# Zero matmuls in three places at the start of a fused attention and MLP kernel

## The chip, the cores and the metric

The kernel runs on one core of a Trainium2 chip. The metric is the device time of one execution in microseconds (us), as the median of several runs. The engines of a core are named as in the profile: PE (TensorE, matmuls; PEld are its weight loads), DVE (VectorE), ACT (ScalarE), POOL (GpSimd) and SP (SyncE, which here only issues DMAs).

## The reference

Two layers follow each other. The first is linear attention with decay, per batch (4) and head (8), over 768 positions with 64 channels. It works in blocks of 64 positions and carries a state from block to block:

```python
for b in range(nb):
    intra = np.einsum('bhic,bhjc->bhij', qb, kb) * Dmask[None]
    intra = np.einsum('bhij,bhjd->bhid', intra, vb)
    inter = np.einsum('bhid,bhde->bhie', qb * lam_pow[None], kv_state)
    out[:, :, sl] = intra + inter
    kb_dec = kb * rev_pow[None]
    kv_state = lam_block[None, :, None, None] * kv_state + np.einsum('bhsd,bhse->bhde', kb_dec, vb)
```

The second is an MLP on the 3072 tokens, with all heads of a token side by side (512 channels), a hidden width of 2048 and an ELU between:

```python
h = x @ w_in
g = np.where(h > 0.0, h, alpha * (np.exp(np.minimum(h, 0.0)) - 1.0))
return (g @ w_out).astype(np.float32)
```

Inputs and the output are fp32.

## The kernel before

The kernel cuts the sequence in six chunks of 128 positions instead of twelve of 64, so there are 24 pieces of work g = 4 c + b (chunk c of batch b), each with all eight heads and 128 tokens. Pieces 0 to 3 go through the MLP alone, later ones in pairs. Arithmetic on PE is fp16 with fp32 sums.

The steps of one piece have one letter each:

- T (att_T_pe, line 262): eight PE transposes turn q and k so that channels are on partitions; DVE multiplies q by the decay on the way out of PSUM (qT, line 278), ACT copies k (kT, line 279).
- S (att_S, line 282): eight matmuls of kT with qT give the scores; DVE multiplies them by the decay mask (pp, line 306).
- P (att_P, line 315): the product with v (line 326) and, for later chunks, with the state (line 332). ACT or DVE copies the sum to xt (line 347 or 349).
- U (att_U, line 376): the state's update from kd (k times decay, made by POOL in att_kd, line 157) and v, written to st by DVE (line 404 or 406); M (att_M, line 356) lets POOL decay the old state (stt, line 366).
- 1:g:j (mm1, line 455): 16 or 8 matmuls of one fourth (or one eighth) of w_in with xt into a bank psH, of which there are two; ACT makes exp and relu of it (lines 472 and 473), DVE joins both to g (line 445).
- 2:g:j (mm2, line 478): four matmuls of g with four slices of w_out, summed in psM; after the last, ACT copies the result (osb) and SP stores it.

The order is written out by hand. Each engine works through its instructions in the order in which the program gives them, and the program runs the tokens of the string OPEN (line 51) in order: first memsets of the states (z, Z), then T0, T1, S0, S1, P0, P1, T2, 1:0:0, S2, 1:1:0, P2, U0, M, 1:2:0, 1:0:1, 2:0:0 and so on. Behind OPEN a small planner places the rest by fixed lags. FIRST (line 50) comes before OPEN and has the cast of q of piece 0 (q0:0) and the decay constants (c0 to c2).

Loads are in POOL_ORDER (line 45), on POOL's DMA queue, which also casts fp32 to fp16: k0, k1, the two iota, q1, k2, v1, i0, v0 and so on, where i0 to i7 are pairs of 128-column slices of w_in and o0 to o7 pairs of 128-row slices of w_out. d0 to d3 in this list are the kd products of POOL, m4 the decay of the first state; POOL works these in order with its DMA issues, so a load behind d0 is issued after d0. q of piece 0 alone comes as fp32 on SP's queue (raw_q, line 105) and is cast by DVE (line 115).

PSUM banks go by name: BANKS (line 62) gives the bank of each early step, and mm1 takes the two banks psH in turn.

What stands ahead of the first PE work on DVE: the casts of iota (lines 204 to 206), the identity matrix (208), the causal mask (211), small copies (216, 217), the cast of q0 (115).

Of the kernel before, what the change touches and what calls it, by code (L numbers as in the profile page):

```python
# [7 lines left out]
FP32 = mybir.dt.float32  # L8
FP16 = mybir.dt.float16
# [6 lines left out]
def kernel(  # L16
# [11 lines left out]
    nc = tc.nc  # L28
# [20 lines left out]
    RAW = "q0"  # L49
    FIRST = "q0:0 c0 c1 c2"  # L50
    OPEN = (
        "z1 z0 z3 Z1 Z2 Z0 z2 T0 T1 S0 S1 P0 P1 T2 1:0:0 S2 1:1:0 P2 U0 M 1:2:0 1:0:1 2:0:0 "
        "1:1:1 2:1:0 1:2:1 T3 2:2:0 1:0:2 S3 1:2:2 2:2:1 2:1:1 P3 1:1:2 1:3:0 2:0:1 2:0:2 "
        "2:1:2 1:1:3 U1 1:2:3 M Z3 2:2:2 1:3:2 U2 1:3:1 2:1:3 1:0:3 T5 T4 2:2:3 1:3:3 S4:5 "
        "2:0:3 2:3:2 2:3:0 M U3 M B:P4:P5:U4:U5 W8 2:3:3 1:4:1 T6 W9 1:4:0 T7 2:3:1 1:4:3 S6:7 "
# [14 lines left out]
    cpool = ctx.enter_context(tc.tile_pool(name="cst", bufs=1))  # L70
    wpool = ctx.enter_context(tc.tile_pool(name="w", bufs=1))
    asb = ctx.enter_context(tc.tile_pool(name="asb", bufs=1))
    msb = ctx.enter_context(tc.tile_pool(name="msb", bufs=1))
    ps = ctx.enter_context(tc.tile_pool(name="ps", bufs=1, space=bass.MemoryType.PSUM))

    lam_b = cpool.tile([128, H], FP32, name="lam_b")
    nc.sync.dma_start(out=lam_b[:], in_=lam.unsqueeze(0).broadcast_to([128, H]))
# [32 lines left out]
    def cast_raw(g, w, eng):  # L110
        n = f"{w}{g}"
        t = asb.tile([128, 1, H, 64], FP16, tag=f"{w}n1", name=f"{w}n{g}", bufs=4)
        (qg if w == "q" else kg)[g] = t
        if eng == 0:
            nc.vector.tensor_copy(t[:, 0], raw[n][:])  # L115
        else:
            nc.scalar.copy(t[:, 0], raw[n][:])
# [164 lines left out]
    def att_S(g):  # L282
        qt, kt = qkT[g]
        psS[g] = [
            bank(f"S{g}", hh, [128, NHP, 128], FP32, f"psS{g}_{hh}") for hh in range(2)
        ]
        for hp in range(NHP):
            for hh in range(2):
                r = slice(hh * 64, (hh + 1) * 64)
                nc.tensor.matmul(  # L290
                    psS[g][hh][:, hp, :], lhsT=kt[r, hp, :], rhs=qt[r, hp, :],
                    start=True, stop=True,
                )
# [7 lines left out]
    def att_E(g):  # L301
        pts = psS.pop(g)

        def half(hh):
            P = asb.tile([128, NHP, 128], FP16, tag="pp", name=f"pp{g}_{hh}", bufs=6)
            nc.vector.tensor_tensor(  # L306
                out=P[:], in0=pts[hh][:], in1=mask[:, hh::2, :], op=ALU.mult
            )
            Pt[(g, hh)] = P
            if hh == 1:  # L310
                E_done.add(g)

        return [lambda: half(0), lambda: half(1)]
# [62 lines left out]
    def att_U(g, pu=None):  # L376

        cb, b = divmod(g, B)
        if cb == NCB - 1:
            return []  # L380
        vt = of(vg, g)
        if pu is None:
            full = bank(f"U{g}", 0, [128, NHP, 128], FP32, f"psU{g}")
            for hp in range(NHP):
                nc.tensor.matmul(
                    full[:, hp, :].rearrange("p (h e) -> p h e", h=2),
                    lhsT=kds[g][:, 2 * hp : 2 * hp + 2, :],
                    rhs=vt[:, 2 * hp : 2 * hp + 2, :], start=True, stop=True,
                )
        else:  # L390
            for hp in range(NHP):
                for hh in range(2):
                    r = slice(hh * 64, (hh + 1) * 64)
                    nc.tensor.matmul(  # L394
                        pu[r, hp, :], lhsT=kds[g][:, 2 * hp + hh, :], rhs=vt[:, 2 * hp + hh, :],
                        start=True, stop=True, skip_group_check=True,
                    )
        new = st[b][(cb + 1) % 2]

        def update(hh):  # L400
            r = slice(hh * 64, (hh + 1) * 64)
            src = full[r, :, r] if pu is None else pu[r, :, :]
            if cb == 0:
                nc.vector.tensor_copy(new[r, :, r], src)
            else:
                nc.vector.tensor_tensor(  # L406
                    out=new[r, :, r], in0=stt.pop((g, hh))[r], in1=src, op=ALU.add
                )
            if hh == 1:
                Y_done.add(g)  # L410

        return [lambda: update(0), lambda: update(1)]

    def burst(*ops):

        us = [int(o[1:]) for o in ops if o[0] == "U" and int(o[1:]) // B < NCB - 1]
        evs, i = [], 0
        for o in ops:
            if o[0] == "P":
                evs += att_P(int(o[1:]))  # L420
            elif int(o[1:]) in us:
                if i == 0:
                    pu = bank(o, 0, [128, 2, NHP, 64], FP32, f"psU{o[1:]}")
                evs += att_U(int(o[1:]), pu[:, i])
                i += 1
        if evs:
            late.insert(0, evs[0])
            late.pop(0)()
            late.extend(evs[1:])
# [91 lines left out]
    def ready(t):  # L521

        g = int(t[1:])
        if t[0] == "P":
            assert g < B or f"U{g - B}" in seen
        if t[0] == "U" and g < 2 * B:
            assert f"{'z' if g < B else 'Z'}{g % B}" in seen
        if t[0] == "U" and g >= B:
            assert f"U{g - B}" in seen and (g < 2 * B or f"P{g - B}" in seen)
        seen.add(t)  # L530

    def run(t):
        w, *a = t[0], *t[1:].replace(":", " ").split()
        if w == "B":
            for o in a:
                ready(o)
            burst(*a)
            return
        a = [int(x) for x in a]
        if w in "PUzZ":  # L540
            ready(t)
        if w == "S":
            for g in a:
                att_S(g)
            for g in a:
                late.extend(att_E(g))
            late.pop(0)()
            late.pop(0)()
        elif w == "P":
            burst(t)  # L550
        elif w == "U":
            late.extend(att_U(*a))
            while late:
                late.pop(0)()
        else:
            {"T": att_T_pe, "1": mm1, "2": mm2, "Z": zero_st, "z": zero_st1,
             "q": lambda g, e: cast_raw(g, "q", e), "k": lambda g, e: cast_raw(g, "k", e),
             "c": lambda i: (emit_qs, emit_mask, emit_ks)[i](), "W": pool_work, "L": load_pair,
             "M": next_M}[w](*a)

    for t in FIRST.split():
        run(t)
# [30 lines left out]
    for x, (g, j) in enumerate(m1):  # L593
# [3 lines left out]
        n = 2  # L597
# [6 lines left out]
    for t in prog:  # L604
        run(t)
# [33 lines left out]
```

## Time and profile before

| what | value |
|---|---|
| median of three runs | 218.0 us (217.15 to 218.4) |
| span of the profiled execution, first to last instruction | 215.9 us |
| the profiled execution's own time beside its span | not given; the median is 2.1 us above the span |
| PE busy | 199.9 us (93%) |
| PEld busy | 138.2 us (64%) |
| DVE and ACT busy | 129.9 and 129.1 us (60% each) |
| POOL busy | 96.2 us (45%) |
| chain that ended last | PE 83%, DMA 7%, POOL 6% |
| PE's idle time before its first instruction | 5.58 us |

The page of a profile gives one execution. Busy time is that in which an engine had an instruction at work; matmuls overlap, so a busy PE isn't yet PE at its peak. The timeline merges neighbouring instructions of one line, operation and shape to a row: start, length, engine, line, what is written from what, the count, and in brackets how long the engine had been idle and what ended it. The chain is followed back from the last instruction: at each step to what released it, or to the instruction before it on its engine. Views of waits give sums of idle time by what ended it. A DMA's time is that from issue to landing.

### The profile page before, as it was taken

To read this page: it belongs to the slowest core of one execution; us is meant where nothing else is said; L and a number is where in the kernel's file an instruction comes from. 1 tells how busy PE (TensorE), PEld (TensorE's weight loads), DVE (VectorE), ACT (ScalarE), POOL (GpSimd) and SP (SyncE) were. 2 spreads that over 40 slices of the span, in tenths; PEclk is the share of its full clock that TensorE was granted. 3 is DMA by queue.
4 is the path that set the end of the run, shared out by engine and by line. 5 is a ranking of instruction groups with operands and counts; after the bars stand their busy time and mean duration, and the time that the engine had idled before them with its cause. 6 is when DMAs were issued, how large, how long until landed. Compare 5 with 4: busy or idle time off the path is not lost.

```text
span 215.9 us, 5095 instructions
## 1 busy us (share of the span) xinstructions
PE 199.9 (93%) x2036; PEld 138.2 (64%) x2036; DVE 129.9 (60%) x223; ACT 129.1 (60%) x245; POOL 96.2 (45%) x115
## 2 busy tenths in 40 slices
PE   0568999999999998999999999999999999999992
PEld 0466676768685675666766766766766666766641
DVE  3926463777837778658657657667667547444410
ACT  4536664884866656665565566476476576566730
POOL 7998890999996419167067159300000000000000
PEclk9999999999999999999999999999999999999999
DMA  8999999999999956989969919999114110111021
GB/s 89 140 173 193 190 144 180 139 169 144 151 156 145 143 126 131 123 109 97 153 114 125 175 58 103 152 181 152 50 59 90 52 49 0 55 49 49 3 92 54
DMA packets 101976, 24.59 MB, mean 114 GB/s; under 512 B 92608, under 2 KB 99008, under 8 KB 101952
## 3 DMA queue, kind: packets, MB, share of 16 engines
q0 software_dynamic: 79760, 13.50, 82.6%
q1 hardware_dynamic: 22192, 10.76, 25.6%
q8 instruction: 16, 0.26, 0.5%
q14 instruction: 8, 0.07, 0.1%
HBM read 27.27 MB, written 6.29 MB: 155 GB/s over the span
## 4 chain that ended last, share of the span: by engine, by line
PE 83%; DMA 7%; POOL 6%; issue 1%; DVE 1%; ACT 0%; SPq 0%; POOLq 0%
PE psM L488 38%; PE psH L466 36%; DMA wo<-in_moe_w_out_dram 4%; DMA kT<-kn 3%; PE psO L326 3%; PE psS L290 3%; PE psO L332 2%; POOL wi L136 1%; POOL kn L97 1%; POOL vn L97 1%; POOL qn L97 1%; PE psT L271 1%; PE psU L394 1%; POOL kd L162 0%; POOL wo L143 0%
## 5 line engine op out<-in xcount | busy, mean ns | idle before, releaser
L466 PE MATMUL psH<-xt,wi 128*128 128x256 f16 (+1 forms) x896 | 99.9, 259 | 1.5 <-DVE g L445 0.8
L445 DVE SCALAR_TENSOR_TENSOR g<-e,psH 128x512 f16<-128x512 f32 x96 | 65.8, 686 | 56.5 <-ACT psH L473 55.9
L488 PE MATMUL psM<-wo,g 128*128 128x512 f16 (+1 forms) x388 | 96.4, 377 | 0.9 <-DVE osb L501 0.5
L472 ACT ACTIVATE e<-psH 128x512 f32<-128x512 f32 x96 | 57.3, 597 | 66.1 <-PE psH L466 62.8
L466 PEld LDWEIGHTS <-wi 128*128 128x128 f16 x896 | 77.8, 99 | 26.8 <-DVE g L445 2.0
L473 ACT ACTIVATE psH<-psH 128x512 f32<-128x512 f32 x96 | 57.0, 594 | 0.0
L488 PEld LDWEIGHTS <-g 128*128 128x128 f16 x388 | 36.3, 98 | 29.9 <-issue 1.3
L306 DVE TENSOR_TENSOR pp<-psS,mask 128x512 f16<-128x512 f32 x48 | 30.9, 684 | 5.3 <-PE psS L290 5.3
L162 POOL TENSOR_TENSOR kd<-kn,ks 128x512 f16<-128x512 f16 x20 | 20.7, 1039 | 18.7 <-DMA kn<-in_k_dram 17.7
L366 POOL TENSOR_TENSOR stt<-st,upp 64x256 f32<-64x256 f16 x32 | 19.5, 608 | 19.8 <-DVE st L406 13.5
L503 ACT COPY osb<-psM 128x512 f32<-128x512 f32 (+1 forms) x24 | 13.9, 581 | 6.3 <-PE psM L488 6.3
L97 POOL DMA_DIRECT2D kn<-in_k_dram x14 | 15.5, 1106 | 0.8 <-POOLq L623 0.8
L97 POOL DMA_DIRECT2D vn<-in_v_dram x14 | 15.5, 1109 | 0.6 <-DMA wi<-in_moe_w_in_dram 0.6
L326 PE MATMUL psO<-pp,vn 128*64 128x128 f16 x192 | 12.4, 230 | 3.0 <-DMA vn<-in_v_dram 2.9
L97 POOL DMA_DIRECT2D qn<-in_q_dram x13 | 14.8, 1139 | 0.0
L406 DVE TENSOR_TENSOR st<-stt,psU 64x256 f16<-64x256 f32 x32 | 13.3, 417 | 1.2 <-PE psU L394 0.5
L326 PEld LDWEIGHTS <-vn 128*64 128x64 f16 x192 | 10.1, 114 | 6.1 <-DMA vn<-in_v_dram 3.1
L349 DVE TENSOR_TENSOR xt<-psO,qs 128x512 f16<-128x512 f32 x16 | 11.0, 688 | 4.1 <-PE psO L332 4.1
L332 PE MATMUL psO<-qT,st 128*64 128x128 f16 x160 | 10.0, 219 | 0.0
L271 PE MATMUL psT<-ident,qn 128*128 128x128 f16 x32 | 3.8, 252 | 6.5 <-DVE qn L115 5.6
L290 PE MATMUL psS<-qT,kT 64*128 64x128 f16 x192 | 8.7, 228 | 0.8 <-DMA kT<-kn 0.7
L332 PEld LDWEIGHTS <-st 128*64 128x64 f16 x160 | 8.9, 110 | 0.0
(38 smaller groups left out, 64.8 us busy)
## 6 DMA issues: line engine op xcount, KB each, us to landing
out_dram<-osb SPq DMA_DIRECT2D x23, 256.0 KB, 2.5
kn<-in_k_dram POOLq DMA_DIRECT2D x10, 256.0 KB, 8.1
qn<-in_q_dram POOLq DMA_DIRECT2D x10, 256.0 KB, 7.1
vn<-in_v_dram POOLq DMA_DIRECT2D x10, 256.0 KB, 8.6
wi<-in_moe_w_in_dram POOLq DMA_DIRECT2D x8, 256.0 KB, 7.4
wo<-in_moe_w_out_dram POOLq DMA_DIRECT2D x8, 256.0 KB, 8.4
kn<-in_k_dram POOLq DMA_DIRECT2D x4, 128.0 KB, 4.3
vn<-in_v_dram POOLq DMA_DIRECT2D x4, 128.0 KB, 6.1
```

Source lines behind the costliest of these rows:

```text
L97: nc.gpsimd.dma_start(out=t[:].rearrange("p b h d -> p (b h) d"), in_=src)
L162: nc.gpsimd.tensor_tensor(out=kd[:], in0=of(kg, g), in1=ks[:].unsqueeze(2).broadcast_to([128, H, 64]), op=ALU.mult,)
L290: nc.tensor.matmul(psS[g][hh][:, hp, :], lhsT=kt[r, hp, :], rhs=qt[r, hp, :], start=True, stop=True,)
L306: nc.vector.tensor_tensor(out=P[:], in0=pts[hh][:], in1=mask[:, hh::2, :], op=ALU.mult)
L326: nc.tensor.matmul(po[r, hp, :], lhsT=vt[:, 2 * hp + hh, :], rhs=Pt[(g, hh)][:, hp, :], start=True, stop=(cb == 0), skip_group_check=True,)
L332: nc.tensor.matmul(po[r, hp, :], lhsT=st[b][cb % 2][:, hp, r], rhs=qt[:, hp, :], start=False, stop=True, skip_group_check=True,)
L366: nc.gpsimd.tensor_tensor(out=tmp[r], in0=old[r, :, r], in1=upp[r].unsqueeze(2).broadcast_to([64, NHP, 64]), op=ALU.mult,)
L445: nc.vector.scalar_tensor_tensor(out=g[:].rearrange("p f c t -> p (f c t)"), in0=e[:], scalar=-1.0, in1=r[:], op0=ALU.add, op1=ALU.min,)
L466: nc.tensor.matmul(pH[:, f * n * 128 : (f + 1) * n * 128], lhsT=wi16[i][:, kk, w * 128 : (w + 1) * 128], rhs=xg[g0][:, kk, :], start=(kk = ...
L472: nc.scalar.activation(e[:], pH[:], AF.Exp)
L473: nc.scalar.activation(pH[:], pH[:], AF.Relu)
L488: nc.tensor.matmul(psM[g][:, cols], lhsT=gts[(g, j * FB + f)], rhs=wo16[i][:, w, cols], start=first and f == 0, stop=end and f == FB - 1, ...
```

## The change

A tile zero16 of 128 x 512 fp16 zeros is made by DVE ahead of everything else that the kernel gives DVE. A function zero_matmuls(n) takes a psH bank and issues n matmuls of 512 columns with zeros as both operands; nothing reads their sums. Ten are issued at the very start, two between T0 and T1 (token w2), and six between S1 and P0 (token w6). All other instructions keep their order.

```diff
     OPEN = (
-        "z1 z0 z3 Z1 Z2 Z0 z2 T0 T1 S0 S1 P0 P1 T2 1:0:0 S2 1:1:0 P2 U0 M 1:2:0 1:0:1 2:0:0 "
+        "z1 z0 z3 Z1 Z2 Z0 z2 T0 w2 T1 S0 S1 w6 P0 P1 T2 1:0:0 S2 1:1:0 P2 U0 M 1:2:0 1:0:1 2:0:0 "
...
     ps = ctx.enter_context(tc.tile_pool(name="ps", bufs=1, space=bass.MemoryType.PSUM))
+
+    zero16 = cpool.tile([128, 512], FP16, name="zero16")
+    nc.vector.memset(zero16[:], 0.0)
+
+    def zero_matmuls(n):
+        z = ps.tile([128, 512], FP32, tag="psH", bufs=2, name="psZ")
+        for _ in range(n):
+            nc.tensor.matmul(z[:], lhsT=zero16[:, 0:128], rhs=zero16[:], start=True, stop=True)
+
+    zero_matmuls(10)
 
     lam_b = cpool.tile([128, H], FP32, name="lam_b")
...
-             "M": next_M}[w](*a)
+             "M": next_M, "w": zero_matmuls}[w](*a)
```

## The prediction

> **What bounds the kernel now.** I read the page first: TensorE (PE) is busy 199.9 of 215.9 us, so the question for a change at the start is whether PE or something else sets the time there. So next came the timeline of the first 31 us (columns: start us, length us, engine, line, operation, tiles, shape, count, and in brackets the idle time before and what ended it):
>
> ```profile
> 5.58 0.61 PE L271 MATMUL psT<-ident,qn 128*128 128x128 f16 x4 [5.58 <-DVE qn L115]
> 7.51 0.61 PE L271 MATMUL psT<-ident,qn 128*128 128x128 f16 x4 [0.90 <-DMA qn<-in_q_dram]
> ...
> 12.70 1.06 PE L326 MATMUL psO<-pp,vn 128*64 128x128 f16 x16 [2.87 <-DMA vn<-in_v_dram]
> ...
> 14.53 1.91 PE L466 MATMUL psH<-xt,wi 128*128 128x128 f16 x16
> ...
> 19.77 2.13 PE L466 MATMUL psH<-xt,wi 128*128 128x128 f16 x32 [0.71 <-ACT xt L347]
> ...
> 22.67 0.59 PE L488 MATMUL psM<-wo,g 128*128 128x512 f16 x2 [0.34 <-DMA wo<-in_moe_w_out_dram]
> ...
> 23.10 1.05 PE L466 MATMUL psH<-xt,wi 128*128 128x128 f16 x16
> ```
>
> Two things are to be seen. PE has three holes, and the change puts zeros in exactly these: 5.58 us ahead of chunk 0, 0.90 ahead of chunk 1 and 2.87 ahead of P0. And PE starts slow: the same 16 matmuls of 128 columns take 1.91 us at 14.53 and 1.05 at 23.10. One slow matmul lasts 0.314 us and a fast one 0.219 (largest and smallest of the tile view of psT), so the step from one start to the next is (1.91 - 0.31)/15 = 0.107 us slow and (1.05 - 0.22)/15 = 0.055 fast. At 19.77 it is already fast. The granted clock reads 1.00 in all stages, so that column does not show the slow phase; the durations do.
>
> Then the chain that ended last, around the end of this stage (start us, length us, what):
>
> ```profile
> 12.57 1.04 POOL kd L162
> 13.61 0.90 POOL qn L97
> 14.51 8.12 DMA wo<-in_moe_w_out_dram
> 22.63 0.04 issue
> 22.67 0.59 PE psM L488 x2
> 23.26 0.89 PE psH L466 x16
> 24.15 0.86 PE psM L488 x4
> 25.02 0.89 PE psH L466 x16
> ```
>
> Up to 22.63 the chain is not PE at all. It is POOL, issuing loads one behind the other, and then the second pair of w_out (o1), issued at 14.51 and landed 8.12 us later; behind 22.67 it is PE, piece against piece. The third matmul of the step 2:0:0 had waited for o1. So a PE that is earlier before 22.67 waits longer there.
>
> Last, whether a later load binds as well: the weight loads between 34 and 37 us, and POOL's own idle time in its first 60 us (us in total, times, longest):
>
> ```profile
> 36.02 0.90 PEld L466 LDWEIGHTS <-wi 128*128 128x128 f16 x16 [0.51 <-DMA wi<-in_moe_w_in_dram]
> ```
>
> ```profile
> POOL stt L366 <- DVE st L404: 5.4, 1, 5.4
> POOL kn L97 <- POOLq L623: 0.8, 1, 0.8
> POOL vn L97 <- DMA wi<-in_moe_w_in_dram: 0.6, 1, 0.6
> POOL kd L162 <- DMA kn<-in_k_dram: 0.5, 1, 0.5
> ```
>
> i6, issued at 27.94 and landed 8.0 us later (35.97), releases the step 1:1:3 at 36.02; PE's matmuls before it run to 36.00. That is a second date that transfers set, with 0.02 us of slack. POOL waits in this time for DMA (queue room, the landing of kn3 ahead of d3) and once for PE's work, 5.4 us up to 37.85, behind the second date. The first 36 us are paced by loads.
>
> **The change part by part.** The memset of zero16 is 1 KB per partition, as those of st: 0.27 us (group of L188, 272 ns). VectorE does nothing before 3.60, where it waits for iota; the memset hides there. Uncovered it would cost 0.27.
>
> The ten matmuls of 512 columns: at the slow step 4 x 0.107 = 0.43 us each, 4.3 in all. Other engines begin at 0.73 (ScalarE, SyncE); a memset from there ends at 1.0 and the block at 5.3, 0.3 before T0's data at 5.58. If it ran over by some tenths, T0's readers are still later: ScalarE's kT copy at 7.18 and VectorE's qT at 7.67 come behind their own queues, while T0 ends at 6.6. Cost 0.
>
> w2: T0's last matmul starts at 6.30, so PE is free at 6.41; two slow ones end at 7.26, T1's data come at 7.47. Cost 0. w6: S1's last pair starts at 9.52, so it runs from 9.63 for 6 x 0.43 = 2.6 us slow (to 12.2) or 6 x 0.22 = 1.3 fast (to 10.9); v lands at 12.66. Cost 0, even at the slow step. The products are ready by then (VectorE's four pp end at 11.6). The tile psZ takes three turns of the two psH banks; PE alone writes it and nobody reads it, so the next psH step waits for no other engine. No DMA is added, moved or held; POOL's and SyncE's queues are the same. 18 matmuls and 18 weight loads more on PE: code loading is not seen to stop PE in this trace, taken at 0.
>
> What a warm clock gives. In this trace the fast step comes near 17.2 us (within the row at 16.91), 4.5 us after PE began to work without long holes at 12.70. By that measure ten zeros (4.3 us) and T0 make it fast by about 6 to 7 us. Now the walk of the changed kernel, with fast pieces from the chain (0.34 per P of 8, 0.45 per T, 0.89 per 16 of mm1, 0.33 per S). P0 and P1 from 12.70 to 13.4. T2 13.5 to 14.0, since q2 lands at 13.49 (issued 7.71, 5.8 us). 1:0:0 half at 14.0, half when i1 lands (8.58 + 6.3 = 14.9), to 15.3; before, 16.2. S2 to 15.7, 1:1:0 to 16.6, P2 behind VectorE's two pp (15.8 + 1.3 = 17.1) to 17.3, U0 to 17.5. xt2 on ScalarE behind four exp and relu of 0.6 (15.5 + 2.4 = 17.9) to 18.5; before, 19.7. 1:2:0 to 19.45, 1:0:1 behind i3 (11.62 + 8.0 = 19.6) to 20.4, the first two of 2:0:0 to 20.9; before, 22.3. So PE gains 1.4 us at this place, of 1.9 that the halved pieces promise (0.5 in P0 and P1, 0.4 in T2, 0.9 in 1:0:0, 0.1 in S2 and the start of 1:1:0). And there it stands until 22.67: the wait for o1 grows from 0.34 to 1.7 us, and this is what is late next. From 22.67 on every piece of PE already runs at 0.86 to 0.89, with nothing slow to win.
>
> Can o1 land earlier? Its issue follows d0 (12.57) and q3 (13.61) on POOL, and POOL asks PE for nothing before stt at 21.84; so no. Can the start of loads move? The first issue at 1.25 waits 0.8 for POOL's own queue. The memset might meet it at SBUF; bounds: below, 0 (it ends 0.2 before), above, its whole 0.27. Taken: 0.
>
> One cost the trace doesn't show is what a wait of 1.7 us does to the fast clock: the longest PE waits while fast are 0.7 and 0.8 us, and behind them the pieces are still 0.87. From above, the slow phase again: 4.5 us at half rate, +2.2 us, as at 12.70 to 17.2. From below, 0. I take 0, since 1.7 is nearer to 0.8 than to the 5.6 us of idle before the slow start.
>
> The Trainium skill, "TensorE: Matmul & The Clock Gate" (Part 1), says that the clock opens after about 3.4 us of sustained work and closes after an idle window of 3.4 us, and that the ramp is worth under 1% of a kernel. It agrees with the steps of 0.107 and 0.055; by it the zeros open the clock and a wait of 1.7 us leaves it open. Its 1%, an estimate from that page, would be 2.2 us off; my sum by the rows is 0, since the loads take it.
>
> Sum: span 215.9 + 0 (zeros and memset) - 1.4 (fast pieces) + 1.4 (longer wait for o1) = 215.9. The three runs have a median of 218.0; the 2.1 between lie outside the span or in the spread of the runs (the profiled execution's own time is not given). Forecast 218.0, no change; its own range is the spread of the runs, 217.2 to 218.6.
>
> **The rivals.**
> (a) The loads come earlier in timed runs than under the profiler. Then the wait for o1 is not there and the 1.4 us show, if i6 lands as much earlier; with half of it, 0.7. For it: the wait is only 0.34, and the profile records every packet. Against: two dates bind one behind the other, and 218.0 leaves no room for a timed run that is much shorter than the profiled one. 216.6.
> (b) The other side: the clock closes in the longer wait for o1 (20.9 to 22.67). PE is the chain from there on, so a second slow phase counts in full: +2.2, 220.2. It decides if 1.7 us of idle suffices to close it. If instead it closes in the 1.8 us before P0, PE is as before and nothing changes.
> (c) The change doesn't do what it says: the zeros do not open the clock (or not for long), the fast step comes near 17 us again. All zeros still fit in their holes: 218.0.
>
> **How the numbers follow.** Forecast 0.62, (c) 0.14, (a) 0.14, (b) 0.10. A median of three or so can be told from no change at about 0.5% (1.1 us). Same: 0.62 + 0.14, less 0.05 for noise on both sides, and 0.03 from the halves of (a) that stay within it: 0.74. Faster: 0.11 of (a) and 0.04 = 0.15. Slower: 0.10 of (b) and 0.01 = 0.11. The range leaves out (b) and the outer half of (a): 216.7 to 218.9, where 218.9 has the 0.27 of the memset above 218.6.
>
> **What would show it.** Right: row times fall in 1:0:0 from 1.91 to about 1.3 with a hole for wi in it; P0 still begins near 12.7; the idle time before the third psM matmul is 1.2 to 2 us, released by DMA wo, at 22.6 again; 1:1:3 at 36.0; span within 0.5 of 215.9. Wrong: psM's third matmul clearly before 22.2 (a), steps of 0.107 behind 22.7 (b), or at 14.5 (c), or P0 later than 12.9, zeros in the way. I'd be wrong altogether if the landings of o1 and i6 moved with PE's work.

## The result

The changed kernel takes 216.96 us (median of 22 executions, 215.59 to 217.93), the kernel before, in executions taken between them, 218.76 (217.0 to 223.66). The ratio of the two is 0.9945, with a 95% interval of 0.9926 to 0.9964; so the change makes the kernel faster by 0.4 to 0.7%, some 1.2 us. The time lies inside the forecast range, but the forecast was "no change". The ratios leave out executions that are more than 1.5% above the fastest of the same kernel, which is why 0.9945 is nearer to 1 than the medians are: of all executions told of here, 21 of 178 of the kernel before and none of 46 of the changed kernel took over 220 us, and in the 17 whose granted clock is on record it had closed for a while (mean 0.992 or less; the last section shows such a closing in profiles of other kernels).

In the executions whose span is on record the time is 1.7 to 2.0 us above it. The two profiled spans are 215.9 before and 215.5 after: one profile of each can't carry a difference of 1.2 us, and this is the difficulty of the whole case.

The timeline of PE in the first 25 us of the changed kernel (start us, length us, engine, line, operation, tiles, count, and in brackets the idle time before and what ended it):

```profile
1.19 4.45 PE L82 MATMUL psZ<-zero 128*128 128x512 f16 x10 [1.19 <-DVE zero L77]
5.58 0.61 PE L281 MATMUL psT<-ident,qn 128*128 128x128 f16 x4
...
6.26 0.59 PE L82 MATMUL psZ<-zero 128*128 128x512 f16 x2
7.83 0.40 PE L281 MATMUL psT<-ident,qn 128*128 128x128 f16 x4 [0.98 <-DMA qn<-in_q_dram]
...
9.46 1.47 PE L82 MATMUL psZ<-zero 128*128 128x512 f16 x6
12.46 0.64 PE L336 MATMUL psO<-pp,vn 128*64 128x128 f16 x16 [1.54 <-DMA vn<-in_v_dram]
...
13.76 0.61 PE L476 MATMUL psH<-xt,wi 128*128 128x128 f16 x8
14.63 0.62 PE L476 MATMUL psH<-xt,wi 128*128 128x128 f16 x8 [0.26 <-DMA wi<-in_moe_w_in_dram]
...
15.51 1.07 PE L476 MATMUL psH<-xt,wi 128*128 128x128 f16 x16
...
20.68 0.62 PE L476 MATMUL psH<-xt,wi 128*128 128x128 f16 x8 [0.63 <-DMA wi<-in_moe_w_in_dram]
...
22.61 0.59 PE L498 MATMUL psM<-wo,g 128*128 128x512 f16 x2 [0.88 <-DMA wo<-in_moe_w_out_dram]
23.04 1.05 PE L476 MATMUL psH<-xt,wi 128*128 128x128 f16 x16
```

The zeros fit in their holes: T0 begins at 5.58 as before, P0 at 12.46 (before 12.70). The clock opens during them: T1's four transposes take 0.40 us (0.61 before) and 1:1:0 takes 1.07. The trace's clock record puts the opening at 6.08 us; in the profile of before it is at 17.18. And the idle time ahead of the third psM matmul has grown from 0.34 to 0.88 us. That matmul starts at 22.61, against 22.67.

The chain there, and the weight loads of 1:1:3:

```profile
13.61 0.90 POOL qn L107
14.50 8.06 DMA wo<-in_moe_w_out_dram
22.56 0.04 issue
22.61 0.59 PE psM L498 x2
23.20 0.89 PE psH L476 x16
24.09 0.86 PE psM L498 x4
```

```profile
35.70 0.95 PEld L476 LDWEIGHTS <-wi 128*128 128x128 f16 x16 [0.26 <-DMA wi<-in_moe_w_in_dram]
```

The same two dates: o1 lands at 22.56 (22.63 before), and the step of i6 begins at 35.7 (36.0). POOL's waits in its first 60 us tell the same, the long one for PE's work is shorter, 4.7 instead of 5.4 us, and the one for queue room longer:

```profile
POOL stt L376 <- DVE st L414: 4.7, 1, 4.7
POOL vn L107 <- DMA wi<-in_moe_w_in_dram: 1.9, 1, 1.9
POOL kn L107 <- POOLq L633: 0.8, 1, 0.8
```

In this pair of profiles, then, the change brings 0.25 us by 36 us (the first matmul of 1:1:3 starts at 35.77 instead of 36.02). Where do 1.2 us come from? PE's next long wait is near 70 us, where the second half of the scores of pieces 10 and 11 waits for kT. kT is made there by a DMA transpose on SP's queue. The waits of PE between 55 and 76 us (us in total, times, longest), before and after:

```profile
PE psS L290 <- DMA kT<-kn: 0.7, 1, 0.7
```

```profile
PE psS L300 <- DMA kT<-kn: 0.5, 1, 0.5
```

### The profile page after: what moved, and what is told of

The parts are those of the page before. It is cut to its first block, busy times and chain, and to the rows that moved or that the text cites. A ratio compares the mean times of both kernels' runs of the same rounds, so it can differ in the third digit from the quotient of the medians.

```text
span 215.5 us, 5132 instructions
## 1 busy us (share of the span) xinstructions
PE 203.4 (94%) x2054; PEld 137.8 (64%) x2054; DVE 130.1 (60%) x224; ACT 129.1 (60%) x245; POOL 96.1 (45%) x115
## 4 chain that ended last, share of the span: by engine, by line
PE 83%; DMA 7%; POOL 6%; issue 1%; DVE 1%; ACT 0%; SPq 0%; POOLq 0%
PE psM L498 38%; PE psH L476 36%; DMA wo<-in_moe_w_out_dram 4%; DMA kT<-kn 3%; PE psO L336 3%; PE psS L300 3%; PE psO L342 2%; POOL wi L146 1%; POOL kn L107 1%; POOL vn L107 1%; POOL qn L107 1%; PE psT L281 1%; PE psU L404 1%; POOL kd L172 0%; POOL wo L153 0%
## 5 line engine op out<-in xcount | busy, mean ns | idle before, releaser
L482 ACT ACTIVATE e<-psH 128x512 f32<-128x512 f32 x96 | 57.3, 597 | 66.4 <-PE psH L476 63.2
L476 PEld LDWEIGHTS <-wi 128*128 128x128 f16 x896 | 77.0, 98 | 27.7 <-DVE g L455 2.0
L107 POOL DMA_DIRECT2D vn<-in_v_dram x14 | 15.5, 1109 | 1.9 <-DMA wi<-in_moe_w_in_dram 1.9
L107 POOL DMA_DIRECT2D kn<-in_k_dram x14 | 15.5, 1106 | 0.8 <-POOLq L633 0.8
L300 PE MATMUL psS<-qT,kT 64*128 64x128 f16 x192 | 8.1, 218 | 0.9 <-DMA kT<-kn 0.5
L357 ACT CAST xt<-psO 128x512 f16<-128x512 f32 x8 | 4.4, 588 | 6.9 <-PE psO L336 4.8
```

The source lines that it names most:

```text
L107: nc.gpsimd.dma_start(out=t[:].rearrange("p b h d -> p (b h) d"), in_=src)
L300: nc.tensor.matmul(psS[g][hh][:, hp, :], lhsT=kt[r, hp, :], rhs=qt[r, hp, :], start=True, stop=True,)
L476: nc.tensor.matmul(pH[:, f * n * 128 : (f + 1) * n * 128], lhsT=wi16[i][:, kk, w * 128 : (w + 1) * 128], rhs=xg[g0][:, kk, :], start=(kk = ...
L482: nc.scalar.activation(e[:], pH[:], AF.Exp)
```

## The experiments

The expectations speak of four theories.

- **A**: the clock opens at another time in each execution. In some of them it opens late, PE and not o1 sets the start of 22.6, and the zeros pay. Otherwise the dates of the loads bind, as forecast.
- **B**: the loads land earlier in timed executions than in profiled ones, so that the early clock shows (rival (a) of the prediction).
- **C**: something else that varies between executions, or noise.
- **D** (formed after the third group): it is not the clock. The added instructions on PE shift the code packets, 16 KB that PE's queue of instructions fetches now and then; the fifth of them, near 61 us, no longer meets the DMA transposes that PE waits for near 70.

Ratios are to the kernel before on the same chip, with 95% intervals, over 10 to 12 executions each (6 for light_after; before_3 and before_4 are one execution each and have no ratio). "Average" below means that of the executions under 220 us, worked out from the single times.

### One part at a time, beside an unchanged kernel

before_again is the kernel before, a measure of the comparison itself. The others are made from the changed kernel:

```diff
 memset_only:  -    zero_matmuls(10)
               -  T0 w2 T1 S0 S1 w6 P0      +  T0 T1 S0 S1 P0
 ten_only:     -  T0 w2 T1 S0 S1 w6 P0      +  T0 T1 S0 S1 P0
 w6_only:      -    zero_matmuls(10)
               -  T0 w2 T1 S0 S1 w6 P0      +  T0 T1 S0 S1 w6 P0
```

> The kernel before, unchanged, as a second sample of its start. Theory A (late opening): the moment at which PE's step falls from 0.107 to 0.055 us differs from execution to execution, and in many it comes later than the 17.2 us of the first profile, by up to some 3 us; PE then passes the landing of o1 and everything behind is late by up to 1 us. Expected: ratio 1.000, the spans of the runs spread over 2 us or more, and a second profile whose fast step does not begin at 17.2 us; if it begins later than about 18, no wait for DMA wo stands ahead of the third psM matmul. Theory B (earlier loads): the fast step begins near 17 us again, and o1 lands clearly before 22.6, by about 1 us. Theory C (noise elsewhere): fast step near 17, o1 near 22.6, and the spans spread for reasons behind 36 us.

> The change without any of its 18 matmuls: only the tile zero16 and its memset remain. Theories A, B and C: ratio 1.000 to the kernel before, within 0.003, since the memset hides in VectorE's idle start; the fast step begins at 16 to 20 us as before. If the gain of 0.55% came from moved tile addresses or code, it would show here: ratio 0.9945. Its profile is another sample of the opening moment.

> Only the ten zeros at the start; no w2 and no w6. The holes of 0.9 us ahead of T1 and of 2.9 us ahead of P0 are then empty. Theory A: the clock opens at 6 to 7 us; whether it stays open through the hole of 2.9 us is open. If it stays, the ratio is about 0.9945, as with the whole change; if it closes, PE is slow again at 12.7 and the ratio is 0.997 to 1.000. Theory B gives the same in both cases, so this run tells which part of the change does the work, not A from B.

> Only the six zeros ahead of P0, at the slow step from 9.6 to 12.2 us. S0 and S1 before them and P0 behind make PE busy without a long hole from 8.5 us on. Theory A: the fast step begins between 12 and 16 us, so PE reaches 2:0:0 before o1 in nearly all executions and nearly the whole gain comes from w6: ratio 0.995 to 0.997, with the spans nearly as close together as in the changed kernel. If the zeros count for little, the fast step begins at 16 to 20 us and the ratio is 1.000.

| kernel | ratio | clock opens at, us | third psM (idle before), us |
|---|---|---|---|
| before_again | 0.9997 [0.9966, 1.0027] | 18.42 | 22.50 (0) |
| memset_only | 0.9984 [0.9955, 1.0014] | 17.59 | 22.79 (0.47) |
| ten_only | 0.9955 [0.9923, 0.9987] | 7.22, closed 10.63 to 17.46 | 22.74 (0.51) |
| w6_only | 0.9936 [0.9913, 0.9958] | 14.20 | 22.40 (0.29) |

The memset alone shows no gain, though its interval leaves room for 0.4%; so I looked to the matmuls. But ten_only, whose clock is closed again when the slow pieces come, seemed to gain, and w6_only seemed to gain as much as all 18. No theory of the early clock gives both. In none of the three kernels with matmuls or memset is the third psM matmul early.

before_again does show a case of theory A. Its clock opened at 18.42 us, 1:1:0 took 1.84 us (1.17 in the profile of before), and the four psM matmuls went through without a wait; o1 had landed at 22.39:

```profile
16.76 1.84 PE L466 MATMUL psH<-xt,wi 128*128 128x128 f16 x16
...
22.07 1.03 PE L488 MATMUL psM<-wo,g 128*128 128x512 f16 x4
```

That execution lost 0.1 us by it, no more.

### The date of o1

```diff
 after_again:   the changed kernel, unchanged
 o1_late:       -  d0 q3 o1 i4 k3           +  d0 q3 i4 o1 k3
 light_before and light_after (of before and after):
                POOL_ORDER without i4 to i7 and o1 to o7
                -  wi_of[...] = (i, j)      +  wi_of[...] = (i % 4, j)
                -  wo_of[...] = (i, j)      +  wo_of[...] = (0, j)
```

> The changed kernel unchanged, beside the other runs on this chip. All theories: ratio 0.9945 within 0.003, spans of the runs within about 2.4 us. Its second profile: the fast step begins at a moment that lies on a grid of 3.41 us, at the end of the first such window that the ten zeros fill: between 4 and 8 us.

> The changed kernel with o1 issued one place later on POOL, behind i4 (some 0.7 us later, landing some 1.2 us later, near 23.8 us by the first profile, where i4 landed). Theory A (the landing of o1 sets the date in timed executions as in the profile): PE is released 1.2 us later and all behind it is late by as much, so about 1.2 us longer than the changed kernel: ratio 0.998 to 1.001. Theory B (loads come earlier in timed executions, so that PE does not wait for o1 there): up to 0.3 us longer than the changed kernel: ratio 0.994 to 0.996.

> The kernel before without eleven weight loads: i4 to i7 and o1 to o7 are not issued, and the first four pairs of w_in slices and the first pair of w_out slices are used in their place; so the computation is not that of the reference. No weight load binds PE any more. Against the kernel before: the waits for o1 and i6 go (0.34 and 0.02 us in the first profile), the queue behind them empties; 0.3 to 1.5 us faster, ratio 0.993 to 0.998. It is the other half of the next run.

> The changed kernel without the same eleven weight loads (the same computation as the run before it). Its distance to that run is what the zeros are worth where no weight load sets a date. Theory A: more than the 1.2 us measured for the change with all loads, since the loads take part of it there: 1.9 us or more for an opening at 17 to 19 us, a ratio between the two of 0.991 or less. Theory B: the loads take nothing in timed executions, so the same 1.2 us, at most 1.5: a ratio between the two of 0.993 to 0.995. In the profile no wait for DMA wo stands ahead of the third psM matmul, and with zeros this matmul begins 1.4 us or more earlier than without.

after_again: 0.9945 [0.9914, 0.9976]; the clock opened at 3.88, o1 landed at 22.04, and PE waited 0.93 us for it. The gain was there again, and the early clock was waiting for o1 again.

o1_late: 1.0008 [0.9968, 1.0047]. With o1 issued 0.75 us later (15.25 us, after 14.50) and landed at 23.24 us (22.56 and 22.04 in the two profiles of the changed kernel) the whole gain is lost, in timed executions. Theory B, by which nobody waits for o1 there, has this against it. PE's timeline and two windows of it (us, PE, PEld, DVE, ACT and POOL busy with counts, PEclk, DMA share, GB/s):

```profile
14.15 1.90 PE L476 MATMUL psH<-xt,wi 128*128 128x128 f16 x16
...
23.28 0.59 PE L498 MATMUL psM<-wo,g 128*128 128x512 f16 x2 [1.08 <-DMA wo<-in_moe_w_out_dram]
```

```profile
10.90:14.30 3.40, 1.36 (x28) 1.09 (x28) 0.71 (x2) 0.99 (x2) 3.33 (x5) 1.00 1.93 163
14.30:17.70 3.40, 3.40 (x37) 2.80 (x35) 1.60 (x3) 1.72 (x4) 3.40 (x6) 0.50 1.43 195
```

The clock had opened and closed again: behind a window in which PE was busy for 1.36 of 3.40 us, ahead of P0, the next goes at half rate (1:0:0 in 1.90 us). Even so o1, at 23.24, is later than PE by 1.08 us. The reading has one blemish: 7 of its 12 executions show such a closing in their mean clock, against 2 of 12 of after_again, so a part of the loss may be the clock's. The five without a closing average 218.05 us (217.4 to 219.6), after_again's ten 217.24: a loss of 0.8 us is left that o1's date has to answer for, as far as five executions can tell.

The light pair leaves out eleven loads and takes the same weights again and again, so both compute something else. Ratios: light_before 1.0003 [0.9972, 1.0033], light_after 0.9894 [0.985, 0.9938]; between the averages of the two lie 1.0%, 2.1 us. I had expected that from 1.4 us at the third psM matmul. The profiles of light_before and light_after show otherwise:

```profile
21.50 1.03 PE L487 MATMUL psM<-wo,g 128*128 128x512 f16 x4
```

```profile
20.78 0.62 PE L475 MATMUL psH<-xt,wi 128*128 128x128 f16 x8 [0.67 <-DMA wi<-in_moe_w_in_dram]
21.24 1.03 PE L497 MATMUL psM<-wo,g 128*128 128x512 f16 x4
```

There is no wait for o1 in either, but i3 had taken its place (landed 20.74): PE is 0.26 us ahead, and 0.5 us at 67 (67.62 and 67.11 for the same four psM matmuls). The rest comes at the next stop, kT near 70 us, for which light_before waited 3.13 us and light_after 0.56. The profiled execution of light_before took 220.94 us, 2.7 above its kernel's average, so this pair shows where time can go and not how much goes there as a rule.

### A date moved forward, and the scatter of the kernel before

```diff
 before_3, before_4:  the kernel before, unchanged
 o1_early:       -  i3 d0 q3 o1 i4 k3       +  i3 d0 o1 q3 i4 k3
 o1_early_w10:   as o1_early, and  -  w6    +  w10
```

> The kernel before once more, for the moment of the opening. Theory A: it lies between 15.5 and 19.5 us and differs from 17.18, 18.42 and 17.59; the third psM matmul starts at o1's landing if the opening is before about 17.9, and behind it without a wait if it is later, by half of the time by which it is later.

> As the run before it: a further moment of opening between 15.5 and 19.5 us, and a wait for o1 only where it is before about 17.9.

> The changed kernel with o1 issued one place earlier on POOL, ahead of q3 (0.9 us earlier, landing near 21.3 instead of 22.1 to 22.6 us). Theory A (the gain of the zeros is cut off at the landing of o1): PE goes on 0.7 to 0.9 us earlier at the third psM matmul, until the next date (1:1:3, i6 landed at 34.6 to 35.7) takes part of it: 0.3 to 0.9 us faster than the changed kernel, ratio to the kernel before 0.990 to 0.993. If the dates of the loads don't bind in timed executions: the ratio stays at 0.9945.

> The run before this one, with ten zeros instead of six ahead of P0, which fills the hole of 1.5 us to 0.7 or less. In this study the clock closed at the end of a 3.41-us window that held 1.8 us or more of idle time, and stayed open with 1.5; so fewer executions should fall back to the slow step at 13 to 17 us (recorded as a mean clock of 0.992 or less). Where o1's date still hides a slow phase, this brings nothing: ratio equal to the run before within 0.002; otherwise up to 0.002 lower.

o1_early 0.9961 [0.9927, 0.9996], o1_early_w10 0.9942 [0.9902, 0.9982]: neither is better than the change alone. The profile of o1_early had lost its early clock ahead of P0 (open at 4.36, closed from 14.6 to 18.02 us), so it can't test o1's date. In o1_early_w10 the third psM matmul begins at 21.96, 0.6 us earlier than in the changed kernel, but then PE waits 0.53 us for another w_out pair at 34.5, and i6 lands at 35.81: 1:1:3 begins at 35.86, where it did anyway. There the second date takes what the first gives.

In before_3 and before_4 the clock opened at 16.46 and 15.51 us. Both waited for o1, 0.42 and 0.36 us, and both for kT near 70: 1.35 and 2.03 us. So theory A holds as to the opening, which varied between 15.5 and 18.4 us in profiles that had no early clock, and fails as to its price: only with an opening at 18.28 or 18.42 us was PE later than o1, by 0.1 to 0.2 us.

What set me on D is the 1:1:3 start. Averaged over profiles with all loads and POOL's order unchanged, it is 35.81 us (34.9 to 36.4) in eight without an early clock and 35.93 (35.2 to 37.2) in five with one at the slow pieces (after, after_again, after_third, w6_only, w6_again; the last profiles are from below). **No gain of the early clock shows by 36 us**, as forecast, though averages that scatter like this could hide some 0.4 us. So I looked behind it, where the two kernels differ by the place of instructions, and by that of tiles if zero16 moves any (memset_only has the tile too, and its 0.9984 [0.9955, 1.0014] settles neither way).

What does differ is the fifth code packet. The 16 packets hold 16 KB each and PE has 4088 instructions in the trace of before, so an instruction is some 64 bytes and a packet some 256 instructions. In all twenty profiles the fifth begins when PE has begun 1204 to 1220 instructions, at whatever time that is. Eighteen matmuls with their weight loads are 36 instructions, 14% of a packet, and the fourth and fifth are 10.2 us apart (51.16 and 61.38 in the trace of before): an estimate of 1.4 us earlier. In the traces the fifth begins at 59.9 to 62.0 us where at most the six of w6 are added, and at 57.5 to 59.2 with all eighteen. The transposes are issued at about 58 (qT) and 59.3 us (kT), and with the early packet they meet nothing. The DMA between 59.5 and 63.4 us, before and then after (GB/s in 40 slices of 0.098 us; queue: packets, MB, share; an issue's median us to landing):

```profile
GB/s 150 144 163 151 169 160 172 190 210 201 226 235 164 131 122 105 166 236 294 436 273 69 203 47 0 0 0 0 3 8 8 8 11 11 8 11 16 365 399 420
...
q8 instruction: 1, 0.02, 1.5%
...
kT<-kn SPq DMA_TRANSPOSE x1, 4.5
```

```profile
GB/s 156 158 160 162 171 183 209 215 213 194 159 112 121 110 144 142 244 278 284 276 200 74 19 3 0 147 168 210 441 357 357 315 357 336 116 207 213 210 226 207
...
q1 hardware_dynamic: 1681, 0.64, 75.9%
q0 software_dynamic: 1002, 0.13, 52.0%
```

Before, q8 (the code packet, 61.38 to 62.33) is in the list, and for thirteen slices, 61.84 to 63.11, next to nothing lands on any queue. In the packets' own records 25 packets of SP's queue (11 of 4 bytes, 6 of 256 and 8 of 2048) begin at 61.66 to 61.82 and end together at 63.1 to 63.2, 1.3 to 1.5 us each, 0.8 us behind the end of the code packet. kT lands 4.5 us after its issue. After, q8 is missing, the hole is three slices long, and the kT of the same issue lands after 2.7 us.

### The same instructions without the clock

```diff
 tiny18, tiny18_again:
-  nc.tensor.matmul(z[:], lhsT=zero16[:, 0:128], rhs=zero16[:], ...)
+  nc.tensor.matmul(z[0:64, 0:16], lhsT=zero16[:, 0:64], rhs=zero16[:, 0:16], ...)
 ten_again:    as ten_only
 after_third:  the changed kernel, unchanged
```

> The changed kernel with its 18 zero matmuls in the same places, but each with a 64-column weight and 16 columns instead of 512, so that PE is hardly busy with them. Theory A (the clock at the start alone): the clock opens at 15.5 to 18.5 us as before, ratio 1.000 within 0.002. Theory D (the 36 instructions move the code packet away from the DMA transposes): in the profile the fifth code packet lies before 59.5 us, qT and kT at 58 to 60 us land after 4.0 and 2.8 us instead of 5.3 and 4.4, and part of the gain is there without a fast start: ratio 0.996 to 0.9985. If D were all of it: 0.9945.

> The run before it once more, for a second profile and as many executions again: A alone 1.000, D in part 0.996 to 0.9985, D alone 0.9945; fewer executions with a closing of the clock near 72 us (mean clock of 0.992 or less) than the kernel before if D holds, since the wait for kT before it becomes shorter.

> The ten zeros alone once more. Their clock opens, closes in the hole ahead of P0 and opens again, so the mean clock of each execution tells how long PE was slow: about 0.983 for two windows of 3.41 us (opening again by 17.6 us) and about 0.976 for three (18 us or later). Theory A: executions of 0.976 take 0.5 to 1.2 us longer than those of 0.983, and those of 0.983 are as fast as the changed kernel's. If the moment of the opening is of no account: no difference.

> The changed kernel on the same chip as the three runs before it: ratio 0.9945 within 0.003; its distance to tiny18 is the part of the gain that the clock brings, with the code in the same place.

| kernel | ratio | clock opens at, us | fifth code packet, us | wait for kT near 70, us |
|---|---|---|---|---|
| tiny18 | 0.9966 [0.9933, 0.9999] | 15.81 | 57.7 | none |
| tiny18_again | 0.9978 [0.9951, 1.0004] | 16.53 | 58.9 | none |
| ten_again | 0.9981 [0.995, 1.0011] | 5.59, closed 9.0 to 15.83 | 59.1 | 0.5 |
| after_third | 0.9976 [0.9947, 1.0006] | 4.78 | 59.2 | 1.02 |

tiny18 adds 36 instructions that cost next to nothing and don't open the clock. In its timeline the pieces are as slow as before, and PE reaches the third psM matmul with o1 just landed:

```profile
1.18 0.70 PE L82 MATMUL psZ<-zero 128*64 128x16 f16 x10 [1.18 <-DVE zero L77]
...
14.48 1.70 PE L476 MATMUL psH<-xt,wi 128*128 128x128 f16 x16
...
21.27 1.10 PE L498 MATMUL psM<-wo,g 128*128 128x512 f16 x4
```

The DMA of tiny18_again between 59.5 and 63.4 us has no code packet, no hole longer than four slices, and the early kT:

```profile
GB/s 133 130 148 150 160 155 159 155 160 158 168 200 198 230 240 199 176 138 76 64 92 63 168 257 278 276 286 98 42 13 0 0 252 84 336 378 294 399 315 399
...
kT<-kn SPq DMA_TRANSPOSE x1, 2.7
```

Together the two runs of it average 217.17 us (24 executions), the kernel before in the same comparison 217.78 (32): 0.9972, and resampling the executions gives 0.9953 to 0.9991. The whole change on that chip, in the same comparison, has 0.9976, and against tiny18 1.0006 (0.9984 to 1.0028). So in this comparison **the 36 instructions without the clock are worth 0.6 us, and the clock adds nothing to it that can be seen** (by the interval, between 0.35 us gained and 0.6 lost). It is one comparison; the next section shows how far two of the same kernel can lie apart. No execution of tiny18 was over 220 us.

ten_again was to test theory A: in executions whose clock had closed again early it should be slower. Its six with a mean clock of 0.976 or less have spans of 215.9 on average, its six others 215.7; no clear difference. ten_only's 0.9955 was not repeated, though the intervals of the two overlap.

### Six instead of eighteen

```diff
 w6_again:  as w6_only
 tiny6:     tiny18's matmul, without zero_matmuls(10) and w2; w6 stays
```

> The six zeros ahead of P0 alone, once more: 12 more PE instructions, clock open near 14 us, code packet within the transposes at 58 to 64 us (qT and kT there take some 5.2 and 4.2 us). Theory D (the code's place is the gain, the clock is eaten by the loads): ratio 0.998 to 1.001, with closings near 72 us in one of ten executions or more, as in the kernel before. Theory A (the early clock brings a part of its own): 0.994 to 0.997 again.

> As the run before it, but each of the six matmuls with a 64-column weight and 16 columns: same instructions, same code places, clock opens at 15.5 to 18.5 us as in the kernel before. Both theories: ratio 0.998 to 1.001, closings near 72 us as in the kernel before, unless the shift by 12 instructions (some 0.5 us) already frees the transposes, which its profile would show by landings of about 4.0 and 2.8 us; then 0.996 to 0.998. The difference to w6_again is the clock alone.

w6_again 1.0001 [0.9963, 1.0038], tiny6 0.9992 [0.9956, 1.0029]. Six zeros do open the clock before the slow pieces (at 10.99 us; 1:0:0's first half in 0.61 us), and PE then waits longer for o1:

```profile
9.79 2.04 PE L82 MATMUL psZ<-zero 128*128 128x512 f16 x6
14.10 0.61 PE L475 MATMUL psH<-xt,wi 128*128 128x128 f16 x8
...
22.08 0.59 PE L497 MATMUL psM<-wo,g 128*128 128x512 f16 x2 [0.81 <-DMA wo<-in_moe_w_out_dram]
```

They show no gain here: an early clock with the code packet left where it was. Their DMA between 59.5 and 63.4 us, w6_again and then tiny6:

```profile
GB/s 180 184 213 227 232 214 187 327 108 166 236 273 273 263 129 45 11 0 0 0 0 8 8 8 11 11 8 11 11 308 357 336 399 441 483 357 166 294 291 281
...
q8 instruction: 1, 0.02, 2.1%
```

```profile
GB/s 154 142 146 147 156 155 160 156 160 160 193 211 228 390 181 153 152 155 221 265 250 110 87 16 0 0 0 11 5 11 8 8 11 11 8 13 265 326 135 255
...
q8 instruction: 1, 0.02, 2.2%
...
kT<-kn SPq DMA_TRANSPOSE x1, 4.5
```

The packet is there, and so is the hole of thirteen slices.

w6_only's 0.9936 stands against this and was not repeated; both runs together are at some 0.997. I take the first for a lucky draw, which is no proof. By the averages, which keep w6_only's execution of 218.92 us, the two are at 0.9952 and 0.9999. So two comparisons of one kernel on one chip lie 0.5 to 0.65% apart, further than their intervals allow, and 0.28% for tiny18, from one comparison, is less sure than its own interval says.

Over all profiles, of the first pair of transposes there kT takes 4.2 to 4.7 us and qT 4.1 to 5.6 where the packet comes at 59.9 to 62.0 (before, before_again, before_3, before_4, memset_only, w6_only, w6_again, tiny6, light_before), and kT 2.7 to 3.7, qT 3.9 to 4.6 where it comes by 59.2 (after, after_again, after_third, o1_late, o1_early, o1_early_w10, light_after, both tiny18); the two kernels with ten zeros lie between, kT at 3.6 and 4.1. The records of single packets say the same: 18 to 28 packets of SP's queue that take over 1 us and nearly all end together, 0.8 to 0.9 us behind the end of the code packet, in eight of the first nine (before_again has none) and in the two kernels with ten zeros (code packets at 60.8 and 59.1); 0 to 6 of them in the other nine. So much regularity from a packet whose place moves by 2.8 us ties the hole to the packet. It goes by the packet's place among the transposes and not by the time alone: ten_again and after_third have it at 59.1 and 59.2 us, with 23 and 2 such packets, and the first pair of transposes is issued at 56.9 and 58.2 us in the one and at 58.4 and 60.6 in the other.

The first pair is not what PE waits for, though; that is the second kT, behind it on the same queue. Its wait averages 0.95 us (0 to 2.03) in the eight profiles with all loads and the packet among the transposes, and 0.58 (0 to 1.91) in the eight with the packet ahead. The direction fits, the ranges overlap.

How much room there is can be read from the starts of PE's matmuls in the twenty profiles. From the start of 1:1:3 to the 71st psM matmul, near 58 us, PE takes 22.63 to 22.65 us in every one. From the 91st, near 72 us, to the last, it takes 139.44 or 139.45 us in eighteen (139.54 in memset_only and 140.11 in o1_early, whose clock had closed). So in these profiles the kernels differ ahead of 1:1:3 and between the 71st and the 91st, where PE waits for kT, and nowhere else. Later code packets meet transposes too (near 98 us in some profiles and near 148 in all, again with 8 to 28 slow packets of SP's queue), and they cost PE nothing. Without a closing there, the stretch from the 71st to the 91st takes 14.29 us on average (13.33 to 15.54) in the nine profiles with all loads and fewer than 18 added matmuls, and 13.84 (13.33 to 14.53) in the seven with 18 or more: 0.45 us, with a standard error of some 0.3. 1:1:3 starts at 35.88 and 35.84 us in the same two groups.

## Why the prediction was right and wrong

**Zeros in their holes: right.** The block ends at 5.64 (forecast 5.3, with T0 none the later), w2 and w6 are done well ahead, P0 starts at 12.46. No cost of the memset shows (0.9984 [0.9955, 1.0014]).

**The fast pieces: right, and a little less.** 1:0:0 ends at 15.25 (15.3), 1:1:0 at 16.6 (16.6), xt2 at 18.2 (18.5). But the second half of 1:0:1 waited for i3 until 20.68, where I had 19.6, so that the first two of 2:0:0 end at 21.73 and not at 20.9: a gain of 0.6 us and not 1.4.

**The wait for o1 takes it: right.** 0.34 became 0.88 us (forecast 1.2 to 2, too long for the same reason), with o1 at 22.56. o1_late speaks for it that this date counts in timed executions, the profile of o1_early_w10 that i6 is the next; w6_again, with an early clock alone, shows no gain.

**"18 matmuls and 18 weight loads more on PE: code loading is not seen to stop PE in this trace, taken at 0": this step failed.** It asked whether code loading stops PE, and no wait of PE in the profiles is put down to it. I didn't ask what else a code packet meets on its way, 50 us further on, when 36 instructions move it by some 2 us. tiny18 puts this term at -0.6 us instead of 0 (-0.28%, by resampling -0.09 to -0.47%), in one comparison. That is half of the 1.2 us by which the forecast was wrong; what the other half is stays open. The list of what the change moves held the DMAs of POOL and SP but not those of PE's instruction queue, though the page of the profile lists it with 16 packets.

The Trainium skill, "Runtime: NRT & Kernel Launch" (section "Instruction fetch mechanics"), says that each engine's instruction buffer is refilled in blocks of 16 KB by its own DMA queue, and that crossing a block is mostly hidden. The 16 packets and 0.26 MB of the profile's page agree; that it is hidden agrees with PE's waits here, but the trace shows kT's transpose at 4.2 to 4.7 us with the packet beside it and 2.7 to 3.7 without.

**The rivals.** (a) has o1_late against it. (b) did not come in the profile: the clock stayed open over 0.88 us of wait. In 8 of the 46 timed executions of the changed kernel a mean clock of 0.988 to 0.992 tells of a closing somewhere; they average 217.2 us, the others 217.1, so it cost nothing that shows. But the reasoning of (b) was nearer than I thought. "1.7 is nearer to 0.8 than to the 5.6 us" was my ground for no cost, and 1.72 us of idle does close the clock when it falls into one window (below). (c) did not come in the changed kernel's profiles; the clock opened at 3.88 to 6.08.

**What stays open.** The change has 0.9945 in two comparisons and 0.9976 in a third, tiny18 0.9972: whether the rest, at most 0.3%, is the clock or chance, the runs do not settle. The hole follows the packet, that much the traces show. That it is what the 0.6 us are made of, and not another effect of the same 36 instructions or of the tile zero16, is argued: a packet was not moved without them, and by how much the second kT, for which PE waits, lands earlier for it stays inside the spread of the profiles. The starts of PE's matmuls do say that a gain can only lie ahead of 1:1:3 or in the wait for kT.

## What to carry to other kernels

An engine made faster ahead of a load's date only waits longer for it: look for the next two dates (here o1 and i6) before you count a gain. An edit that adds instructions also shifts every later instruction fetch of that engine, so list its packets among the DMAs that move and look at which of them meets a transfer that somebody waits for. To separate an effect from the mere presence of its instructions, put the same number of instructions there at no work (tiny18); without that run all of the gain here would have been put down to the clock.

## What the runs showed of the hardware

**Half an idle window closes the clock.** The granted clock changes at the ends of windows of 3.41 us (in each profile its changes lie whole multiples of that apart), and their start is not tied to that of the kernel: the same kernel opened at 15.5 to 18.4 us. memset_only in three such windows:

```profile
68.80:72.20 3.40, 1.64 (x24) 0.93 (x22) 2.93 (x5) 0.90 (x2) 3.17 (x5) 1.00 1.74 214
72.20:75.60 3.40, 3.40 (x16) 2.15 (x15) 1.56 (x3) 1.79 (x4) 0.58 (x1) 0.50 0.64 71
75.60:79.00 3.40, 3.40 (x63) 2.38 (x60) 1.21 (x2) 2.59 (x5) 0.00 (x0) 1.00 0.38 109
```

PE was idle for 1.76 us of the first, all of it one wait for kT; the next window goes at 0.50, 16 matmuls instead of 63, and the profiled span is 218.6 us. o1_early closed likewise (1.91 us idle), and o1_late (2.04 of 3.40, above). By PE's busy time, every window of the open clock with 1.72 us idle or more closed it (ten_again, from 5.59 to 9.00 us, has the 1.72), and none with 1.71 or less did (after_third, from 11.60 to 15.01 us, has the 1.71); half of 3.41 is 1.71. before_4's wait of 2.03 us did not, as it fell into two windows as 1.36 and 0.67. A wait of under 2 us so costs nearly 2 us more, in some executions, and whether it does depends on where the window's end falls. The page "TensorE: Matmul & The Clock Gate" (Part 1) of the Trainium skill, as the prediction cites it, has the clock close after an idle window of 3.4 us; the runs show that half of one suffices, and the measurement decides.

**DMA transposes stall behind a code packet.** Where the 16 KB of PE's instructions are fetched while SP's queue works at a transpose, some twenty of SP's packets, of 4, 256 and 2048 bytes, take 1.0 to 1.8 us each and nearly all end at one moment, 0.8 to 0.9 us behind the packet of code (ten profiles), and the other queues land next to nothing for over 1 us (before, w6_again and tiny6 above: thirteen slices of 0.098 us). In before_again such a meeting shows none of it. What it is that they share was not tried.

**The column of the granted clock is blind at the start.** It reads 1.00 before the first opening, while matmuls take twice as long; only the durations and the steps between starts show the slow phase.
